# Attention and a Fourier mixing layer in one kernel: the end of an attention unit in three steps, and the sums of stage 2 on GpSimd

## The chip, the core and the metric

The kernel runs on one core of a Trainium2 chip. The metric is the device time of one execution in microseconds; the kernel before has a median of 2939.95 us in 3 runs (2938.06 to 2941.15). The engines of the core are called PE (TensorE: matmuls), DVE (VectorE), ACT (ScalarE), POOL (GpSimd) and SP (the engine whose queue issues the DMAs here).

## The reference

Two layers on inputs of 2048 positions and 1024 columns; their outputs stand side by side.

```python
# A: 32 heads of 32 columns; one k and one v for all heads
q = heads(x @ wq); k = x @ wk; v = x @ wv
p = softmax(einsum("bhqd,bkd->bhqk", q, k) * 32 ** -0.5)
a_out = concat_heads(einsum("bhqk,bkd->bhqd", p, v)) @ wo
# B: Real(DFT_seq(DFT_hidden(x)))
a = einsum("bsd,ed->bse", x, dft_hid_re); b = einsum("bsd,ed->bse", x, dft_hid_im)
b_out = einsum("ts,bse->bte", dft_seq_re, a) - einsum("ts,bse->bte", dft_seq_im, b)
return concatenate([a_out, b_out], axis=-1)
```

## The kernel before

Every large product in float32 is made of three matmuls in the type fp32r: each operand is split into a high part (a cast) and a low part (operand less its high part), and the product is high x high, high x low, low x high. The names are `mh` and `ml` for the left operand, `rh` and `rl` for the right one. Such a product of 128 x 512 over 1024 rows is a group (class `Group`): 24 matmuls into one PSUM bank `psb`, and at its end `post`.

All groups stand in one list: the projections to k, v and q, stage 1 of the Fourier layer (along the hidden axis), stage 2 (along the sequence) and the projection with `wo`. The function `take(n)` issues the next n matmuls of this list; they fill PE while the attention runs. Around them the planner (`pump`, class `Line`) issues loads on SP, sums of two left operands on GpSimd (`comb`, tiles `m`), casts and subtractions, each a fixed number of matmuls ahead of its use.

Stage 2 uses a scheme with seven products in place of eight (`PRODUCTS`), each in two halves of eight groups. The first half is put aside in a tile `h` by ACT. At the end of a group of the second half (`post` in `stage2`, line 467) DVE adds the PSUM bank to `h`; then `h` is added to or subtracted from each partial result `y` that was loaded from DRAM (line 472), and SP stores it (line 473). A product has one or two such targets beside new ones; 48 of the 56 groups have at least one sum.

The attention runs in 32 units (a block of 512 queries, four heads) of 32 steps. In the main loop (line 680) a step n does four things. `score_step`: two matmuls give 128 x 1024 scores in PSUM (`pss`, two buffers), DVE reduces them to the negative maximum of each row (`nm`), and ACT takes the exponential of the scores one step back, of which only the row sum is kept, and which frees the buffer. `expo`: two matmuls give transposed scores (`pst`, one buffer), ACT writes their exponential to `p`. Every eighth step `pv`: 16 matmuls multiply `p` with `v` into a PSUM bank, and DVE adds it to `ov`. `level`: `take` of so many matmuls that the filling runs out evenly. The last of a unit's four `pv` (lines 623 to 634) also ends the unit: `ov` is multiplied by 1/sum (`rb`), cast to the high part `oh`, and the low part `ol` is the difference; SP stores both for the projection with `wo`.

Each engine works in the order of the program. `Ordered` keeps that order, so a step's place in the code is its place in every engine's queue. The buffers touched here: `ov`, `oh`, `ol` and `rb` one each, `y` four, `h` eight (one for each group of a half), `m` three and two.

Of the kernel before, what the change touches and what calls it, by code (L numbers as in the profile page):

```python
# [8 lines left out]
F32 = mybir.dt.float32  # L9
# [59 lines left out]
def tile_kernel(ctx: ExitStack, tc, xT, wq, wkv, wo, xbT, wT, cT, out):  # L69
# [3 lines left out]
    dve = Ordered(tc, nc.vector)  # L73
    gp = Ordered(tc, nc.gpsimd)
    sp = Ordered(tc, nc.sync)
# [9 lines left out]
    oh_d = [dram.tile([NG, P, W], F32, name=f"oh_{b}") for b in range(NQ)]  # L85
    ol_d = [dram.tile([NG, P, W], F32, name=f"ol_{b}") for b in range(NQ)]
# [27 lines left out]
    def move(q, to, of):  # L114
        q.dma_start(to.bitcast(F32), of.bitcast(F32))
# [152 lines left out]
    def bank(name, open_=False):  # L268

        b = 1 - cur["bank"] if cur["bank"] is not None else int(used[1] < used[0])  # L270
        cur["at"] += 1
        used[b] = cur["at"]
        if open_:
            cur["bank"] = b
        return ps_b[b].tile([P, W], F32, name=name)
# [40 lines left out]
    def aside():  # L316

        j = pos["fill"] % 24
        if pos["fill"] >= len(groups) * 24 or j == 0:
            return  # L320
        if j < 6:
            take(6 - j)
        elif j > 17:
            take(24 - j)
# [32 lines left out]
    ready = set()  # L357
# [73 lines left out]
    def right_of(k, s):  # L431
        assert (k, s) in ready
        return NAMES[k][s]

    def stage2():
        seen, total = {}, {}
        for _, _, outs in PRODUCTS:
            for t, e, _ in outs:
                total[t, e] = total.get((t, e), 0) + 1
        for mt, nt, outs in PRODUCTS[1:] + PRODUCTS[:1]:  # L440
            for half in range(2):
                R = [Item([(lambda s=s, nt=nt: right_of(tuple(nt), s), 1)]) for s in range(half * 8, half * 8 + 8)]
                for k in range(8):
                    left = []
                    for q in range(2):
                        s0 = half * 8 + q * 4
                        left.append(Item([(lambda a=a, k=k, s0=s0: cT[a[0], a[1] * 8 + k, :, s0:s0 + 4], a[2]) for a in mt]))
                    if half == 0:
                        def post(ps, k=k):
                            hs[k] = hp.tile([P, W], F32, name=f"h{k}")  # L450
                            act.activation(hs[k], ps, AF.Copy)
                        yield Group(left, R, post)
                        continue
                    ys = []
                    plan = []
                    for t, e, sg in outs:
                        n = seen.get((t, e, k), 0)
                        seen[t, e, k] = n + 1
                        it = None
                        if n:  # L460
                            it = Item([(lambda t=t, e=e, k=k: y_d[t][e][k], 1)])
                            ys.append(it)
                        r0 = (t * 8 + k) * P
                        to = out[r0:r0 + P, D + e * W:D + (e + 1) * W] if n + 1 == total[t, e] else y_d[t][e][k]
                        plan.append((sg, it, to))

                    def post(ps, k=k, plan=plan):
                        h = hs[k]
                        dve.tensor_add(h, h, ps)
                        for sg, it, to in plan:  # L470
                            if it is not None:
                                (dve.tensor_add if sg > 0 else dve.tensor_sub)(it.y, it.y, h)
                                sp.dma_start(to, it.y)
                            elif sg > 0:
                                sp.dma_start(to, h)
                            else:
                                o = op.tile([P, W], F32, name="qh")
                                act.activation(o, h, AF.Copy, scale=-1.0)
                                sp.dma_start(to, o)
                    yield Group(left, R, post, ys=ys)  # L480


# [41 lines left out]
    units = [(b, g) for b in range(NQ) for g in range(NG)]  # L524
    SU = 32
    LEAD = 12
    total = SU * len(units)
    qst, nm, ls, lse, pt, ov, rb, pend = ({} for _ in range(8))

    def open_unit(u):  # L530
        b, g = units[u]
        assert ("q", b, g) in ready
        q = qsp.tile([P, 4, W], F32R, name="qst")
        gp.memset(q[96:P].bitcast(F32), 0.0)
        for r, src in enumerate((qh_d, ql_d, qh_d)):
            move(sp, q[r * DH:(r + 1) * DH], src[b][g].rearrange("(h d) c -> d h c", d=DH))
        qst[u] = q
        nm[u] = sm.tile([P, 2, NC], F32, name="nm")
        ls[u] = sm.tile([P, 2, NC], F32, name="ls")

    def scores(s):
        u, r = divmod(s, SU)
        i, j = divmod(r, 2)
        h, t = divmod(i, 4)
        ps = ps_s.tile([P, 2 * W], F32, name="pss")
        for a in range(2):
            k0 = (2 * j + a) * W
            te.matmul(ps[:, a * W:(a + 1) * W], qst[u][:, h, t * P:(t + 1) * P], kst[:, k0:k0 + W], start=True, stop=True)
        dve.tensor_reduce(nm[u][:, j, i:i + 1], ps, axis=AX.X, op=ALU.max, negate=True)
        pend[s] = ps  # L550

    def row_sums(s):
        if s not in pend:
            return
        ps = pend.pop(s)
        u, r = divmod(s, SU)
        i, j = divmod(r, 2)
        act.activation(ps, ps, AF.Exp, bias=nm[u][:, j, i:i + 1], accum_out=ls[u][:, j, i:i + 1])
# [9 lines left out]
    def lse_1b(u):  # L568
        act.activation(lse[u][1], lse[u][1], AF.Exp)
# [30 lines left out]
    def expo(n):  # L600
        u, r = divmod(n, SU)
        c, hp_ = divmod(r, 2)
        if hp_ == 0:
            pt[u, c] = pp.tile([P, 4, W], F32, name="p")
        ps = ps_t.tile([P, 2, W], F32, name="pst")
        for a in range(2):
            te.matmul(ps[:, a], kst[:, c * P:(c + 1) * P], qst[u][:, 2 * hp_ + a], start=True, stop=True)
        act.activation(pt[u, c][:, 2 * hp_:2 * hp_ + 2], ps, AF.Exp)

    def pv(u, k):  # L610

        aside()
        ps = bank("psb")
        for c in range(4 * k, 4 * k + 4):
            for h in range(4):
                te.matmul(ps[h * DH:(h + 1) * DH], v[:, c], pt[u, c][:, h], start=c == 4 * k, stop=c == 4 * k + 3)
        if k == 0:
            ov[u] = onp.tile([P, W], F32, name="ov")
            dve.tensor_copy(ov[u], ps)
        else:  # L620
            dve.tensor_add(ov[u], ov[u], ps)
        cur["at"] += 1
        if k == NC // 4 - 1:
            b, g = units[u]
            hi_ = onp.tile([P, W], F32R, name="oh")
            lo_ = onp.tile([P, W], F32R, name="ol")
            dve.tensor_mul(ov[u], ov[u], rb[u])
            dve.tensor_copy(hi_, ov[u])
            dve.tensor_sub(lo_, ov[u], hi_.bitcast(F32))
            lse["out"] = hi_, lo_  # L630
            if u + 1 < len(units):
                move(sp, oh_d[b][g], hi_)
                move(sp, ol_d[b][g], lo_)
            ready.add(("o", b, g))

    def score_step(s):

        if s < total:
            u, r = divmod(s, SU)
            if r == SU - 6 and u + 1 < len(units):  # L640
                open_unit(u + 1)
            scores(s)
        row_sums(s - 1)
        u, e = divmod(s - SU, SU)
        if 0 <= u < len(units):
            if e == 1:
                lse_1(u)
            elif e == 2:
                lse_1b(u)
            elif e == 3:  # L650
                lse_2(u)
            elif e == 5:
                lse_3(u)
# [26 lines left out]
    for n in range(total):  # L680
        u, r = divmod(n, SU)
        if n == total - 12:
            w1 = wo_set(1)
            add([o_group(NQ - 1, t, e, ws) for e, ws in ((0, w0), (1, w1)) for t in range(4)])
        score_step(n + SU + LEAD)
        expo(n)
        if r == 16:
            inverse(u)
        if r % 8 == 0 and n:
            pv(*divmod(n // 8 - 1, 4))  # L690
        level(n + 1)


    last = groups[len(groups) - 8:]
    take((len(groups) - 8) * 24 - pos["fill"] - 12)
    pv(len(units) - 1, 3)
    hi7, lo7 = lse["out"]
    take((len(groups) - 8) * 24 - pos["fill"])

# [58 lines left out]
```

## Time and profile before

| | us |
|---|---|
| median of 3 runs | 2939.95 |
| the profiled execution | 2945.72 |
| its span, first to last instruction | 2943.9 |
| PE busy | 2862.6 (97%) |
| ACT busy | 2273.9 (77%) |
| DVE busy | 2043.3 (69%) |
| POOL busy | 379.2 (13%) |

The granted clock of TensorE was 0.998 of full speed over the span. The profile gives each instruction's engine, start and duration, and for idle time what ended it. Matmuls overlap in a pipeline and their ends are modelled, so the time from one matmul's start to the next one's start tells more than their busy time. All instructions of the kernel are recorded on one line (L50, the helper that keeps the order), so they are told apart by their tiles. About 180 us are projections to k, v and the first q before the attention begins; stage 1 runs from 550 to 1170 us, stage 2 from there to 2620 us, the projection with `wo` after it.

### The profile page before, as it was taken

The page shows a single profiled execution, that of the slowest core. Times are in us where ns is not written, and L with a number is a line of the kernel's source. Part 1 is how long each engine was busy: PE and PEld are TensorE (multiplying, and loading weights), DVE is VectorE, ACT ScalarE, POOL GpSimd, SP SyncE. Part 2 cuts the span into 40 slices and gives each one's busy share as a digit, 9 for nine tenths or more (in the row PEclk, how much of TensorE's full clock was granted, in tenths as well). Part 3 has the DMA queues.
Part 4 walks back from the last instruction along what each step waited for, and adds up shares of the span by engine and source line. Part 5 has one row for each costly group of instructions (what it writes and reads, how often), then busy time and mean ns, then how long its engine had stood idle before and what let it go on. Part 6 is the DMA issues. An engine that isn't in the chain of part 4 may idle for free.

```text
span 2943.9 us, 39970 instructions
## 1 busy us (share of the span) xinstructions
PE 2862.6 (97%) x14096; PEld 1953.1 (66%) x14096; DVE 2043.3 (69%) x2657; ACT 2273.9 (77%) x3342; POOL 379.2 (13%) x278
## 2 busy tenths in 40 slices
PE   8999999999999999999999999999999999999999
PEld 5776666666666666666666666666666666666666
DVE  6866677655555556787788787788888787875511
ACT  4688888787888888877877877878878778788851
POOL 0000000011122223222222220002222200000000
PEclk9999999999999999999999999999999999999999
DMA  8854555455666767445355453254454432454455
GB/s 303 281 195 162 171 171 188 157 174 178 197 209 210 230 212 225 125 149 157 104 166 156 131 168 112 94 173 139 133 158 139 137 119 84 144 160 128 133 145 175
DMA packets 318025, 485.03 MB, mean 165 GB/s; under 512 B 33664, under 2 KB 98688, under 8 KB 317824
## 3 DMA queue, kind: packets, MB, share of 16 engines
q1 hardware_dynamic: 317824, 482.48, 51.4%
q8 instruction: 111, 1.82, 0.2%
q14 instruction: 90, 0.74, 0.1%
HBM read 351.54 MB, written 129.76 MB: 163 GB/s over the span
## 4 chain that ended last, share of the span: by engine, by line
PE 55%; DVE 10%; ACT 5%; issue 1%; DMA 1%; POOL 0%; SPq 0%; ACTq 0%; POOLq 0%; DVEq 0%
PE psb L50 36%; PE pst L50 11%; PE pss L50 9%; DVE nm L50 4%; ACT p L50 2%; ACT pss L50 2%; DVE ov L50 1%; DVE ml L50 1%; DVE y L50 1%; DVE h L50 1%; DVE ol L50 1%; DVE rl L50 1%; DMA m<-in_cT_dram 0%; DVE oh L50 0%; DVE mh L50 0%
## 5 line engine op out<-in xcount | busy, mean ns | idle before, releaser
L50 DVE TENSOR_REDUCE nm<-pss 128x1 f32<-128x1024 f32 x1024 | 1249.1, 1221 | 377.9 <-PE pss L50 374.9
L50 ACT ACTIVATE p<-pst 128x1024 f32<-128x1024 f32 x1024 | 1054.1, 1029 | 387.5 <-PE pst L50 381.1
L50 ACT ACTIVATE pss<-pss,nm 128x1024 f32<-128x1024 f32 x1024 | 1118.5, 1092 | 172.8 <-DVE nm L50 165.1
L50 PE MATMUL psb<-rh,mh 128*128 128x512 f32 (+1 forms) x1916 | 755.4, 394 | 8.6 <-ACT rh L50 8.2
L50 PE MATMUL psb<-rh,ml 128*128 128x512 f32 (+1 forms) x1916 | 755.6, 394 | 0.1
L50 PE MATMUL psb<-rl,mh 128*128 128x512 f32 (+1 forms) x1916 | 754.9, 394 | 0.3 <-DVE rl L50 0.3
L50 PE MATMUL pss<-kst,qst 128*128 128x512 f32 x2048 | 661.6, 404 | 33.5 <-ACT pss L50 32.4
L50 PE MATMUL pst<-qst,kst 128*128 128x512 f32 x2048 | 665.2, 406 | 24.4 <-ACT p L50 23.2
L50 PEld LDWEIGHTS pss<-kst,qst 128*128 128x128 f32 x2048 | 369.1, 188 | 237.3 <-issue 87.2
L50 PEld LDWEIGHTS pst<-qst,kst 128*128 128x128 f32 x2048 | 364.3, 188 | 176.1 <-ACT p L50 101.8
L50 PE MATMUL psb<-p,v 128*32 128x512 f32 x4096 | 466.0, 595 | 1.2 <-DVE h L50 1.2
L50 PEld LDWEIGHTS psb<-rh,mh 128*128 128x128 f32 (+1 forms) x1916 | 359.4, 188 | 96.4 <-ACT rh L50 8.7
L50 PEld LDWEIGHTS psb<-rl,mh 128*128 128x128 f32 (+1 forms) x1916 | 359.3, 188 | 87.0 <-DVE rl L50 1.6
L50 PEld LDWEIGHTS psb<-rh,ml 128*128 128x128 f32 (+1 forms) x1916 | 359.3, 188 | 86.0 <-issue 0.6
L50 POOL TENSOR_TENSOR m<-m,m 128x512 f32<-128x512 f32 x160 | 218.2, 1364 | 872.7 <-DMA m<-in_cT_dram 681.4
L50 PEld LDWEIGHTS psb<-p,v 128*32 128x32 f32 x4096 | 120.0, 109 | 277.3 <-issue 264.8
L50 DVE TENSOR_TENSOR ov<-ov,psb 128x512 f32<-128x512 f32 x96 | 66.0, 688 | 289.3 <-PE psb L50 289.3
L50 ACT ACTIVATION_READ_ACCUMULATOR pss<-pss,nm 128x1 f32 x1024 | 214.5, 210 | 0.0
L50 DVE TENSOR_TENSOR ml<-m,mh 128x512 fp32r<-128x512 f32 (+1 forms) x274 | 208.4, 761 | 4.2 <-ACT mh L50 3.9
L50 POOL MEMSET qst<- 32x2048 f32 x32 | 58.0, 1817 | 843.4 <-PE pst L50 676.9
L50 DVE TENSOR_TENSOR rl<-r,rh 128x512 fp32r<-128x512 f32 x196 | 145.6, 744 | 4.2 <-ACT rh L50 3.2
L50 DVE CAST mh<-m 128x512 fp32r<-128x512 f32 x267 | 132.1, 495 | 7.6 <-DMA m<-in_wq_dram 6.1
(63 smaller groups left out, 698.1 us busy)
## 6 DMA issues: line engine op xcount, KB each, us to landing
m<-in_cT_dram SPq DMA_DIRECT2D x384, 256.0 KB, 3.6
r<-r SPq DMA_DIRECT2D x112, 256.0 KB, 3.7
mh<-xb SPq DMA_DIRECT2D x96, 256.0 KB, 3.9
ml<-xb SPq DMA_DIRECT2D x96, 256.0 KB, 4.2
y<-y SPq DMA_DIRECT2D x96, 256.0 KB, 2.9
y<-r SPq DMA_DIRECT2D x80, 256.0 KB, 2.9
r<-y SPq DMA_DIRECT2D x80, 256.0 KB, 2.0
qst<-qh SPq DMA_DIRECT2D x64, 256.0 KB, 5.8
```

Source lines behind the costliest of these rows:

```text
L50: return lambda *a, **k: self.tc.keep_in_program_order(f(*a, **k))
```

## The change

In `pv` the three instructions at a unit's end are no longer issued at once: they go into a list `ends`, and the main loop issues one of them in each of the next three steps, behind `score_step`. The stores and the mark that the unit is ready go with the last. After the loop what is left is issued at once (the last unit). In `post` of stage 2 the sums into `y` go from DVE to GpSimd.

```diff
@@ post of stage2
-                                (dve.tensor_add if sg > 0 else dve.tensor_sub)(it.y, it.y, h)
+                                (gp.tensor_add if sg > 0 else gp.tensor_sub)(it.y, it.y, h)
                                 sp.dma_start(to, it.y)
@@ pv
             hi_ = onp.tile([P, W], F32R, name="oh")
             lo_ = onp.tile([P, W], F32R, name="ol")
-            dve.tensor_mul(ov[u], ov[u], rb[u])
-            dve.tensor_copy(hi_, ov[u])
-            dve.tensor_sub(lo_, ov[u], hi_.bitcast(F32))
             lse["out"] = hi_, lo_
-            if u + 1 < len(units):
-                move(sp, oh_d[b][g], hi_)
-                move(sp, ol_d[b][g], lo_)
-            ready.add(("o", b, g))
+
+            def low():
+                dve.tensor_sub(lo_, ov[u], hi_.bitcast(F32))
+                if u + 1 < len(units):
+                    move(sp, oh_d[b][g], hi_)
+                    move(sp, ol_d[b][g], lo_)
+                ready.add(("o", b, g))
+
+            ends.append(lambda: dve.tensor_mul(ov[u], ov[u], rb[u]))
+            ends.append(lambda: dve.tensor_copy(hi_, ov[u]))
+            ends.append(low)
@@ main loop
         score_step(n + SU + LEAD)
+        if ends:
+            ends.pop(0)()
         expo(n)
@@ after the main loop
     pv(len(units) - 1, 3)
+    while ends:
+        ends.pop(0)()
     hi7, lo7 = lse["out"]
```

PE's order of instructions stays as it was. On DVE, at the end of the 22nd unit (2050 us in the trace of before), the order was this:

```order
L50 TENSOR_TENSOR ov<-ov,psb 128x512
L50 TENSOR_TENSOR ov<-ov,rb 128x512
L50 CAST oh<-ov 128x512
L50 TENSOR_TENSOR ol<-ov,oh 128x512
L50 TENSOR_REDUCE nm<-pss 128x1
L50 TENSOR_TENSOR ml<-m_18112,mh 128x512
L50 TENSOR_REDUCE nm<-pss 128x1
```

With the change it is this (a number behind `m` or `r` only tells one tile from another):

```order
L50 TENSOR_TENSOR ov<-ov,psb 128x512
L50 TENSOR_REDUCE nm<-pss 128x1
L50 TENSOR_TENSOR ov<-ov,rb 128x512
L50 TENSOR_TENSOR ml<-m_18112,mh 128x512
L50 TENSOR_REDUCE nm<-pss 128x1
L50 CAST oh<-ov 128x512
L50 CAST mh<-m_18157 128x512
L50 CAST rh<-r_18155 128x512
L50 TENSOR_REDUCE nm<-pss 128x1
L50 TENSOR_TENSOR ol<-ov,oh 128x512
```

The next reduction stands right behind the add into `ov`, and each of the three instructions stands behind one of the next reductions, ahead of that step's conversions.

At the end of the first group of stage 2 that has a sum (1490 us in the trace of before), DVE had:

```order
L50 TENSOR_TENSOR h_12427<-h_12427,psb 128x512
L50 TENSOR_TENSOR y_13229<-y_13229,h_12427 128x512
L50 TENSOR_TENSOR ml<-m_13198,mh 128x512
L50 TENSOR_REDUCE nm<-pss 128x1
L50 CAST mh<-m_13252 128x512
```

On GpSimd the change puts the sum between two sums of left operands:

```order
 L50 TENSOR_TENSOR m_13154<-m_13154,m_13156 128x512
 L50 TENSOR_TENSOR m_13198<-m_13198,m_13200 128x512
+L50 TENSOR_TENSOR y_13229<-y_13229,h_12427 128x512
 L50 TENSOR_TENSOR m_13252<-m_13252,m_13254 128x512
 L50 TENSOR_TENSOR m_13329<-m_13329,m_13331 128x512
+L50 TENSOR_TENSOR y_13354<-y_13354,h_12565 128x512
```

The row of `y` leaves DVE, where `ml` now follows `h`; on GpSimd the sum waits for `h`, and `m_13252`, which DVE casts two rows behind `ml`, stands behind the sum.

## Rows read from the trace of the kernel before

**Rows 1.** The page: its busy sums, and DVE in 40 slices
```profile
PE 2862.6 (97%) x14096; PEld 1953.1 (66%) x14096; DVE 2043.3 (69%) x2657; ACT 2273.9 (77%) x3342; POOL 379.2 (13%) x278
...
DVE  6866677655555556787788787788888787875511
```

**Rows 2.** Timeline at a unit's end: start, duration, engine, instruction, [idle before]
```profile
2049.46 0.69 DVE L50 TENSOR_TENSOR ov<-ov,psb 128x512 f32<-128x512 f32 x1 [3.08 <-PE psb L50]
...
2050.19 0.69 DVE L50 TENSOR_TENSOR ov<-ov,rb 128x512 f32<-128x512 f32 x1
...
2050.91 0.43 DVE L50 CAST oh<-ov 128x512 fp32r<-128x512 f32 x1
...
2051.37 0.69 DVE L50 TENSOR_TENSOR ol<-ov,oh 128x512 fp32r<-128x512 f32 x1
2051.53 0.63 PE L50 MATMUL pss<-kst,qst 128*128 128x512 f32 x2
...
2051.98 1.22 DVE L50 TENSOR_REDUCE nm<-pss 128x1 f32<-128x1024 f32 x1
2051.99 0.63 PE L50 MATMUL pst<-qst,kst 128*128 128x512 f32 x2
...
2053.30 1.09 ACT L50 ACTIVATE pss<-pss,nm 128x1024 f32<-128x1024 f32 x1 [1.71 <-DVE nm L50]
2053.38 0.39 PE L50 MATMUL psb<-rh,mh 128*128 128x512 f32 x1
...
2053.61 0.39 PE L50 MATMUL psb<-rl,mh 128*128 128x512 f32 x1
...
2054.55 0.73 PE L50 MATMUL pss<-kst,qst 128*128 128x512 f32 x2 [0.56 <-ACT pss L50]
...
2055.47 0.73 PE L50 MATMUL pst<-qst,kst 128*128 128x512 f32 x2 [0.18 <-ACT p L50]
```

**Rows 3.** Timeline of PE at the first and the thirtieth unit end
```profile
249.11 0.40 PE L50 MATMUL psb<-rh,ml 128*128 128x512 f32 x1
249.81 0.73 PE L50 MATMUL pss<-kst,qst 128*128 128x512 f32 x2 [0.30 <-ACT pss L50]
...
2743.21 0.39 PE L50 MATMUL psb<-rh,mh 128*128 128x512 f32 x1
2744.15 0.73 PE L50 MATMUL pss<-kst,qst 128*128 128x512 f32 x2 [0.56 <-ACT pss L50]
```

**Rows 4.** Groups by form: count | busy us, mean ns | idle before
```profile
L50 POOL TENSOR_TENSOR m<-m,m 128x512 f32<-128x512 f32 x160 | 218.2, 1364 | 872.7 <-DMA m<-in_cT_dram 681.4 <-DVE nm L50 70.9 <-DVE rl L50 31.1
...
L50 POOL TENSOR_TENSOR y<-y,qh 128x512 f32<-128x512 f32 x48 | 62.5, 1302 | 246.1 <-ACT qh L50 232.9 <-DMA qst<-qh 13.1
...
L50 DVE TENSOR_TENSOR y<-y,h 128x512 f32<-128x512 f32 x64 | 47.2, 758 | 1.6
```

**Rows 5.** Timeline in stage 2: additions on GpSimd, and a group's end with one sum
```profile
1484.10 1.23 DVE L50 TENSOR_REDUCE nm<-pss 128x1 f32<-128x1024 f32 x1
...
1484.59 1.30 POOL L50 TENSOR_TENSOR m<-m,m 128x512 f32<-128x512 f32 x1 [5.42 <-DMA m<-in_cT_dram]
...
1489.87 0.68 DVE L50 TENSOR_TENSOR h<-h,psb 128x512 f32<-128x512 f32 x1
...
1490.58 0.69 DVE L50 TENSOR_TENSOR y<-y,h 128x512 f32<-128x512 f32 x1
...
1490.67 1.75 POOL L50 TENSOR_TENSOR m<-m,m 128x512 f32<-128x512 f32 x1 [4.78 <-DVE h L50]
...
1491.19 1.78 DVE L50 TENSOR_TENSOR ml<-m,mh 128x512 fp32r<-128x512 f32 x1
...
1492.89 1.21 DVE L50 TENSOR_REDUCE nm<-pss 128x1 f32<-128x1024 f32 x1
...
1494.54 0.39 PE L50 MATMUL psb<-rh,ml 128*128 128x512 f32 x1
...
1495.45 0.73 PE L50 MATMUL pss<-kst,qst 128*128 128x512 f32 x2 [0.53 <-ACT pss L50]
```

More of the change, by code (lines that the diff above doesn't have):

```diff
@@ L528, in tile_kernel @@
     qst, nm, ls, lse, pt, ov, rb, pend = ({} for _ in range(8))
+    ends = []
     def open_unit(u):
```

## The prediction

> **What bounds the kernel now.** I read the page first: PE is busy 97% of the span, DVE 69%, and DVE's tenths rise from 5 and 6 in the middle to 7 and 8 in the second half of the slices [rows 1]. PE's order of instructions is the same in both kernels, so only PE's waits can change the end. The second view was the timeline about a unit's end. At 2049.46 DVE adds the last product into `ov`, and then does product, cast and subtraction one behind the other; the reduction of the next scores, whose matmuls were long done, starts at 2051.98, 1.83 us after the add's end at 2050.15. ACT's exponential over those scores stands idle 1.71 us for it, and then PE stands, because both buffers of `pss` are taken [rows 2]. I count PE's loss from start to start, since the ends of matmuls are modelled: a `psb` matmul starts 0.23 after the one before (2053.38 to 2053.61), but `pss` starts 0.94 after it (2053.61 to 2054.55), 0.71 too late; `pst` follows `pss` after 0.46 when nothing waits (2051.53 to 2051.99), here after 0.92, another 0.46 [rows 2]. A unit's end costs PE 1.17 us there.
>
> **Unit ends.** The same picture stands at 30 of the 32 ends; the last two lie where the work of filling has ended or nearly so. The part before `pss` is 0.47 at the first (249.11 to 249.81, less 0.23) and 0.71 at the thirtieth (2743.21 to 2744.15) [rows 3]; over the thirty it lies between 0.47 and 1.71, mean 0.83. The part before `pst` is the 0.46 of the worked case each time. So 30 x (0.83 + 0.46) = 38.6 us of PE's time hang on these three DVE instructions.
> The change keeps the add in its place and puts the reduction straight behind it; product (0.69), cast (0.43) and subtraction (0.69) [rows 2] come one each behind the next three reductions. The 1.83 us of delay thereby falls to nothing at the reduction where it hurts. What can come late instead is the next one: a step lasts 2.31 us on PE (2051.53 to 2053.84, if the next `pss` had followed at 0.23), a reduction and the largest piece take 1.22 + 0.69 = 1.91, and 0.40 is left for the conversions of the filling work, a cast and a subtraction (0.43 + 0.69 = 1.12) in a full step. A full step then ends 0.72 late. The reduction that came 1.83 late cost 0.71 before `pss`, so about 1.12 of lateness is free; one full step is within that, two in a row are not quite. I take nine tenths of the 38.6, 35 us. The bounds: nothing (the lateness only moves) and all 38.6, and I take a value near the upper one because the piece and its delay are seen in the rows, and the thirty ends are alike in stages where DVE has room and where it has little.
> The two stores `oh` and `ol` move on SP's queue behind the loads that the next three steps issue; that lets those loads go out before SP waits for `oh`. What reads them comes units later, so I cost it at nothing; if they came late, output groups near the end would wait.
>
> **The sums into y.** Of 56 groups that end a half in stage 2, 48 have such a sum: 32 one, 16 two, 64 in all. On DVE one takes 758 ns on average; GpSimd has the like addition in stage 1 at 1302 ns, and its additions of `m` take 1364 [rows 4]. DVE is relieved of 64 x 0.758 = 48.5 us, GpSimd takes on 64 x 1.30 = 83 us, which its 13% share [rows 1] holds with ease. What this is worth on PE is seen at the groups' ends: at 1489.87 `h` is added, `y` follows, then `ml`, and the reduction behind them starts at 1492.89; `pss` then starts 0.91 after the matmul before it, 0.68 too late [rows 5]. Read so, the PE starts in the 3 to 7 us behind the 48 additions of `h` are late by 27 us in all, between nothing and 1.77 us each. Part of that belongs to the add of `h`, which stays, and to `ml`.
> For `ml` shows the price of GpSimd: begun at 1491.19 beside GpSimd's addition of 1490.67, it took 1.78 us, where the subtraction of the same form at the unit's end took 0.69 [rows 2, 5], and it ended half a microsecond behind GpSimd's. GpSimd's addition itself, begun while DVE summed `y`, took 1.75 instead of 1.30. The reduction of 1484.10, beside GpSimd's addition of 1484.59, kept its 1.23 [rows 5]. So two additions from SBUF stand in each other's way, and a reduction from PSUM does not.
> The Trainium skill, page "SBUF — State Buffer", section "Who interferes with whom", says that a DVE instruction with two SBUF inputs contends with a GpSimd instruction that reads SBUF, and that the one that issues second waits for the whole instruction of the first, while a reduction never contends. By that rule a sum on GpSimd locks DVE's subtractions and casts for longer than the sum took on DVE. The durations of rows 5 agree with it, and it makes the slower rival below possible.
> After the change a sum begins as `h` ends, at once or behind the `ml` that DVE starts first; its 1.30 us lie beside the reduction (1.21) where that comes next, and then DVE loses little. Where casts and subtractions come next, DVE loses what it had saved. And GpSimd keeps its order: the addition of the next `m` now stands behind the sum, and the cast that needs this `m` stands in DVE's order before the next reduction. At ten places DVE's order reads `h`, `ml`, reduction, cast of just that `m`: `ml` and reduction end 0.69 + 1.21 = 1.90 after `h`, GpSimd's sum and addition end 0.69 + 1.30 + 1.30 = 3.29 after it, so the cast waits 1.4 us and the next reduction is 1.8 us late with the cast, like a unit's end: 10 x 1.29 = 13 us. The bounds of this part are thus 27 us gained and 13 us lost, with more in the slower rival. The nearest row is the one of 1490, where relief and new wait about cancel; I take 6 us gained. SP's stores of `y` go out 0.6 us or more later each, with the loads behind them, which are issued several us ahead of their use: nothing.
>
> **The sum.** 35 + 6 = 41 us off the profiled execution's 2945.72 (span 2943.9 and 1.8 around it): 2904.7. The median of the runs lies 5.8 us below that execution, so 2939.95 - 41 = 2899.
>
> **Rivals.**
> 1. The sums on GpSimd give nothing back and the wait for `m` takes their place at the ten places: 35 - 13 = 22 us gained, 2918. For it: the order and the 1.78 us of `ml`. Against: at these places PE pays already today.
> 2. The unit's pieces only move the lateness where DVE is full. 17 of the 30 ends lie in stage 2, so 17 x 1.29 = 22 us stay: 38.6 - 22 = 17 us gained, 2923. For it: DVE's 7 and 8 tenths there. Against: with the wait gone the reduction has 1.12 us of free lateness in each step.
> 3. Both parts give all: 38.6 + 27 = 66, 2874. Against: the add of `h` stays on DVE.
> 4. Rivals 1 and 2 together: 17 - 13 = 4 us gained, which cannot be told from no change (0.2%, 5.9 us, is about what a measurement can tell).
> 5. Slower, by GpSimd's hold on DVE: at each of the 48 places two GpSimd additions in a row (2.60 us) keep DVE's subtraction or cast standing, and the next reduction is 2.60 late, 1.48 beyond the free 1.12, plus 0.46 before `pst`: 48 x 1.94 = 93 us, less the 27 paid there now and the 35 of the unit ends: 31 us slower, 2971. It decides from the point where these places cost over 35 us more than now, 0.73 us each. For it: `ml` of rows 5. Against: at 28 of the 48 places the order has an instruction that reads PSUM right behind `h` (19 times the reduction, which was not held up).
>
> **Chances.** My forecast 0.65, with a range of its own of 2888 to 2910 (unit ends 30 to 38, sums -1 to 14); rival 1 0.14; rival 2 0.07; rival 3 0.05; rival 4 0.04; rival 5 0.05. The range that leaves out rivals 4 and 5, half of rival 3 and part of rival 2 is 2882 to 2923. Faster: 0.65 + 0.14 + 0.07 + 0.05, less 0.01 for their edges, 0.90; no change 0.05; slower 0.05.
>
> **What would show it.** Unit ends right: in the timeline the reduction starts straight behind the add into `ov`, ACT's 1.71 is gone, and PE's `pss` and `pst` follow at 0.23 and 0.46 there; wrong if the same waits stand two or three steps later. Sums right: GpSimd's `y` at about 1.3 us 64 times, reductions behind `h` earlier, few casts of `m` that wait for GpSimd; wrong if idle time of DVE put down to GpSimd's `m` grows to over 10 us, or if the subtractions' mean rises. The forecast fails if PE's busy share does not rise or DVE's waits turn up as waits of PE elsewhere.

## The result, and the profile after

The changed kernel takes 2895.55 us in the median of 4 runs (2893.22 to 2897.75), against 2940.55 of the kernel before on the same occasion: a ratio of 0.9848, 95% interval [0.9831, 0.9865], or 45 us less. The forecast was 2899. The profiled execution took 2893.22 (span 2891.4).

The busy sums of the page, to be read against [rows 1]: PE is busy 23 us less for the same matmuls (a pair that waits is recorded as 0.73 us, one that runs on as 0.63), DVE is relieved of 48, GpSimd took on 89.

```profile
PE 2839.5 (98%) x14096; PEld 1957.6 (68%) x14096; DVE 1995.0 (69%) x2593; ACT 2279.2 (79%) x3342; POOL 467.8 (16%) x342
```

Who waited for whom, first in the kernel before (total us, times, longest):

```profile
ACT pss L50 <- DVE nm L50: 165.1, 145, 4.0
...
PE pss L50 <- ACT pss L50: 32.4, 49, 2.4
```

and after the change:

```profile
ACT pss L50 <- DVE nm L50: 95.2, 111, 3.5
...
DVE mh L50 <- POOL m L50: 15.1, 11, 2.5
...
PE pss L50 <- ACT pss L50: 11.7, 16, 1.9
```

ACT waits 70 us less for DVE's reductions, and PE 21 us less for the buffers of `pss`; one wait has grown, DVE's for GpSimd's `m`, from 1.3 us in 2 times to 15.1 in 11.

The end of the same unit as in [rows 2], in the timeline of the changed kernel (start, duration, engine, instruction):

```profile
2011.06 0.69 DVE L50 TENSOR_TENSOR ov<-ov,psb 128x512 f32<-128x512 f32 x1 [3.08 <-PE psb L50]
...
2011.69 1.22 DVE L50 TENSOR_REDUCE nm<-pss 128x1 f32<-128x1024 f32 x1
...
2012.83 0.68 DVE L50 TENSOR_TENSOR ov<-ov,rb 128x512 f32<-128x512 f32 x1
2012.89 0.39 PE L50 MATMUL psb<-rl,mh 128*128 128x512 f32 x1
...
2013.08 1.08 ACT L50 ACTIVATE pss<-pss,nm 128x1024 f32<-128x1024 f32 x1
2013.12 0.63 PE L50 MATMUL pss<-kst,qst 128*128 128x512 f32 x2
...
2013.58 0.63 PE L50 MATMUL pst<-qst,kst 128*128 128x512 f32 x2
...
2014.03 1.22 DVE L50 TENSOR_REDUCE nm<-pss 128x1 f32<-128x1024 f32 x1
...
2015.16 0.42 DVE L50 CAST oh<-ov 128x512 fp32r<-128x512 f32 x1
2015.20 0.40 PE L50 MATMUL psb<-rl,mh 128*128 128x512 f32 x1
...
2015.43 0.63 PE L50 MATMUL pss<-kst,qst 128*128 128x512 f32 x2
...
2015.90 0.63 PE L50 MATMUL pst<-qst,kst 128*128 128x512 f32 x2
...
2017.30 0.69 DVE L50 TENSOR_TENSOR ol<-ov,oh 128x512 fp32r<-128x512 f32 x1
```

The reduction begins at 2011.69, as the add into `ov` ends, not 1.83 us after it. ACT goes on to the scores at 2013.08 without idle time. PE starts `pss` 0.23 after the matmul before it, in this step and the next (2012.89 to 2013.12, 2015.20 to 2015.43), and `pst` 0.46 and 0.47 behind. Product, cast and subtraction stand behind one reduction each (2012.83, 2015.16, 2017.30) and nobody waits for them. In the 3 to 7 us behind the add into `ov` no start of PE is late at any of the thirty ends, where before each lost 0.93 us or more.

The first group of stage 2 with a sum, the place of [rows 5], has come out as the order promised, and not to the good:

```profile
1466.66 0.68 DVE L50 TENSOR_TENSOR h<-h,psb 128x512 f32<-128x512 f32 x1
...
1467.25 0.69 DVE L50 TENSOR_TENSOR ml<-m,mh 128x512 fp32r<-128x512 f32 x1
...
1467.42 1.68 POOL L50 TENSOR_TENSOR y<-y,h 128x512 f32<-128x512 f32 x1 [11.48 <-DVE h L50]
...
1467.86 1.22 DVE L50 TENSOR_REDUCE nm<-pss 128x1 f32<-128x1024 f32 x1
...
1469.06 2.53 POOL L50 TENSOR_TENSOR m<-m,m 128x512 f32<-128x512 f32 x2
...
1470.38 1.50 DVE L50 CAST mh<-m 128x512 fp32r<-128x512 f32 x1 [1.30 <-POOL m L50]
...
1471.79 1.21 DVE L50 TENSOR_REDUCE nm<-pss 128x1 f32<-128x1024 f32 x1
...
1474.36 0.73 PE L50 MATMUL pss<-kst,qst 128*128 128x512 f32 x2 [0.33 <-ACT pss L50]
...
1475.39 0.73 PE L50 MATMUL pst<-qst,kst 128*128 128x512 f32 x2 [0.30 <-ACT p L50]
```

`h` ends at 1467.34, GpSimd's sum begins at 1467.42 and is held up by DVE's `ml` (1.68 us, not 1.30), then come two additions of `m` (2.53 us for both). DVE has done its reduction by 1469.0, stands idle 1.30 us for the first `m`, and the cast then takes 1.50 us beside the second addition where others take 0.42. The next reduction is late, and PE waits 0.33 before `pss` and 0.30 before `pst`.

Left operands' subtractions and casts on DVE, first before the change (count | busy us, mean ns | idle before):

```profile
L50 DVE TENSOR_TENSOR ml<-m,mh 128x512 fp32r<-128x512 f32 x272 | 207.6, 763 | 3.3 <-ACT mh L50 3.0
...
L50 DVE CAST mh<-m 128x512 fp32r<-128x512 f32 x267 | 132.1, 495 | 7.6 <-DMA m<-in_wq_dram 6.1 <-POOL m L50 1.3 <-PE psb L50 0.2
```

and after, with GpSimd's sums:

```profile
L50 DVE TENSOR_TENSOR ml<-m,mh 128x512 fp32r<-128x512 f32 x272 | 197.3, 726 | 3.6 <-ACT mh L50 3.2
L50 DVE CAST mh<-m 128x512 fp32r<-128x512 f32 x267 | 145.2, 544 | 21.6 <-POOL m L50 15.1 <-DMA m<-in_wq_dram 6.0 <-DMA ql<-ql 0.3
...
L50 POOL TENSOR_TENSOR y<-y,h 128x512 f32<-128x512 f32 x64 | 91.7, 1443 | 564.8 <-DVE h L50 505.9 <-DMA rb<-r 43.7 <-DMA m<-in_cT_dram 15.2
```

A sum takes 1443 ns with its waits for DVE, more than the 1302 of [rows 4]. The subtractions have become shorter in the mean, the casts longer by 49 ns, with 14 us more of idle time before them. Counted over the DVE instructions that ran beside the 64 sums, these took 6.5 us more in all than the medians of their kinds, where DVE was relieved of 48; 45 of the sums lay beside a reduction.

### The profile page after: what moved, and what is told of

The parts are those of the page before. It is cut to its first block, busy times and chain, and to the rows that moved or that the text cites. A ratio compares the mean times of both kernels' runs of the same rounds, so it can differ in the third digit from the quotient of the medians.

```text
span 2891.4 us, 39967 instructions
## 1 busy us (share of the span) xinstructions
PE 2839.5 (98%) x14096; PEld 1957.6 (68%) x14096; DVE 1995.0 (69%) x2593; ACT 2279.2 (79%) x3342; POOL 467.8 (16%) x342
## 4 chain that ended last, share of the span: by engine, by line
PE 45%; issue 6%; DVE 4%; ACT 3%; DMA 3%; POOL 2%; SPq 0%; POOLq 0%; ACTq 0%
PE psb L50 29%; PE pst L50 9%; PE pss L50 8%; DVE nm L50 2%; DMA y<-y 1%; ACT p L50 1%; POOL y L50 1%; ACT pss L50 1%; DVE mh L50 1%; DMA m<-in_cT_dram 1%; SPq L50 0%; DVE ml L50 0%; DMA y<-r 0%; DVE rl L50 0%; POOL m L50 0%
## 5 line engine op out<-in xcount | busy, mean ns | idle before, releaser
L50 DVE TENSOR_REDUCE nm<-pss 128x1 f32<-128x1024 f32 x1024 | 1250.6, 1222 | 361.9 <-PE pss L50 358.8
L50 PE MATMUL pss<-kst,qst 128*128 128x512 f32 x2048 | 657.5, 402 | 12.4 <-ACT pss L50 11.7
L50 DVE TENSOR_TENSOR ml<-m,mh 128x512 fp32r<-128x512 f32 (+1 forms) x274 | 198.1, 723 | 4.0 <-ACT mh L50 3.6
L50 POOL TENSOR_TENSOR y<-y,h 128x512 f32<-128x512 f32 x64 | 91.7, 1443 | 564.8 <-DVE h L50 505.9
L50 DVE CAST mh<-m 128x512 fp32r<-128x512 f32 x267 | 145.2, 544 | 21.6 <-POOL m L50 15.1
```

Of the source, the lines that this page charges most:

```text
L50: return lambda *a, **k: self.tc.keep_in_program_order(f(*a, **k))
```

## The experiments

All ratios are to the kernel before on the same occasion, from 5 rounds each; 0.001 is 3 us. The changed kernel has 0.9848. An interval reaches some 4 us to either side, so the difference of two ratios is open by some 6 us. e6 and e9 add `h` twice and e10 stores zeros, so their Fourier output is not the kernel's; they stand here for their time.

| run | what it is | median us | ratio, 95% interval |
|---|---|---|---|
| e1 | unit ends spread, sums on DVE | 2905.48 | 0.9877 [0.9862, 0.9892] |
| e2 | sums on GpSimd, unit ends in one piece | 2933.19 | 0.9968 [0.9955, 0.9980] |
| e3 | e1 with the three pieces as a lump behind the reduction | 2920.49 | 0.9923 [0.9909, 0.9936] |
| e4 | changed kernel, sums issued behind the next m | 2889.88 | 0.9821 [0.9808, 0.9835] |
| e5 | changed kernel, pieces ahead of the reductions | 2904.93 | 0.9877 [0.9863, 0.9890] |
| e6 | changed kernel, every sum twice | 2917.84 | 0.9921 [0.9908, 0.9935] |
| e7 | e4, preparation of 1/sum in two steps | 2887.02 | 0.9815 [0.9802, 0.9829] |
| e8 | changed kernel, groups with one sum back on DVE | 2895.78 | 0.9843 [0.9829, 0.9856] |
| e9 | e4, every sum twice | 2897.62 | 0.9851 [0.9838, 0.9865] |
| e10 | changed kernel, three memsets behind each sum | 2921.32 | 0.9932 [0.9920, 0.9945] |
| e11 | e7, second sum of a group 12 matmuls later | 2890.20 | 0.9822 [0.9808, 0.9835] |

**e1 and e2: each part alone.** e1 is the changed kernel with

```diff
-                                (gp.tensor_add if sg > 0 else gp.tensor_sub)(it.y, it.y, h)
+                                (dve.tensor_add if sg > 0 else dve.tensor_sub)(it.y, it.y, h)
```

and e2 the kernel before with the opposite edit.

> The unit's end in three steps, the sums into y left on DVE. Theory A (the unit ends carry the gain): 35 to 38 us faster than before, about 2903; the starts of PE behind the 30 unit ends are no longer late. Theory B (the two parts need each other: with y on DVE the pieces only move the lateness in stage 2): 17 us faster, about 2923, with PE late two or three steps behind the 17 unit ends of stage 2.

> The sums into y on GpSimd, the unit's end left in one piece. Theory A: 6 to 10 us faster than before, about 2932, and the unit ends cost PE 1.29 us each as before. Theory B: close to nothing, 2940, since the gain of the sums only comes with room at the unit ends. Rival (GpSimd holds DVE up): slower than before.

e1 gained 36 us and e2 9; their sum, 45.6, is the whole change's 44.7. Theory A holds: the parts do not need each other, and the unit ends carry four fifths. In e1 PE's waits for `pss` are already nearly those of the changed kernel, with DVE nearly as loaded as before (2032 us busy):

```profile
PE pss L50 <- ACT pss L50: 13.2, 17, 2.7
```

In e2 the unit ends cost what they did: in the 3 to 7 us behind the thirty adds into `ov` PE starts 41 us late in all, 42 in the kernel before, none in the changed one.

**e3: is it the spreading, or only the place behind the reduction?**

```diff
-            ends.append(lambda: dve.tensor_mul(ov[u], ov[u], rb[u]))
-            ends.append(lambda: dve.tensor_copy(hi_, ov[u]))
-            ends.append(low)
+            def all_three():           # product, cast and low() in one step
...
+            ends.append(all_three)
```

> Sums on DVE; the unit's three instructions go together, as one lump, behind the next reduction, and are not spread. If what counts is only that the first reduction goes ahead of them: as e1, about 2903. If the lateness allowed in a step is about 1.12 us, as I worked out: the second reduction comes late by the lump less the room of a step, 1.83 - 0.40 and more where conversions stand there, so that about half of the ends lose again some 0.5 to 1.3 us: about 12 us less gain than e1, 2915.

By the ratios it loses 14 us of e1's gain. At a unit's end in stage 2 the timeline shows the old wait one step later:

```profile
1685.16 0.69 DVE L50 TENSOR_TENSOR ol<-ov,oh 128x512 fp32r<-128x512 f32 x1
...
1686.11 0.42 DVE L50 CAST rh<-r 128x512 fp32r<-128x512 f32 x1
...
1686.44 1.22 DVE L50 TENSOR_REDUCE nm<-pss 128x1 f32<-128x1024 f32 x1
...
1687.76 1.09 ACT L50 ACTIVATE pss<-pss,nm 128x1024 f32<-128x1024 f32 x1 [1.41 <-DVE nm L50]
...
1689.01 0.73 PE L50 MATMUL pss<-kst,qst 128*128 128x512 f32 x2 [0.40 <-ACT pss L50]
```

The lump's subtraction is followed by the step's two casts, the reduction begins at 1686.44, ACT has stood idle 1.41 us, and PE waits 0.40 before `pss`. So the place gives some three fifths of the gain and the spreading the rest.

**e5: how much lateness of a reduction is free?** The list is served ahead of `score_step`, so that each piece stands in front of its step's reduction.

```diff
-        score_step(n + SU + LEAD)
         if ends:
             ends.pop(0)()
+        score_step(n + SU + LEAD)
         expo(n)
```

> As the changed kernel, but each of the three pieces stands ahead of its step's reduction and not behind it: each reduction of three is then late by 0.69, 0.43 and 0.69 us. If about 1.12 us of lateness of a reduction is free, as I worked out from the rows of before: no more than 3 us slower than the changed kernel, some 2897, and no waits of PE at the unit ends. If every delay of a reduction costs PE: 30 x (0.2 to 0.5 us) in each of up to three steps, 15 us or more slower, 2910.

It came out between the two, 9 us slower than the changed kernel. Counted by PE's starts, the excess stands in the steps behind a unit's end: in steps 2 to 7 of the units PE starts 24 us late in all, 14 in the changed kernel. An end early in the run shows how:

```profile
329.38 0.69 DVE L50 TENSOR_TENSOR ov<-ov,rb 128x512 f32<-128x512 f32 x1
...
329.99 1.22 DVE L50 TENSOR_REDUCE nm<-pss 128x1 f32<-128x1024 f32 x1
...
331.30 1.09 ACT L50 ACTIVATE pss<-pss,nm 128x1024 f32<-128x1024 f32 x1 [0.52 <-DVE nm L50]
...
332.40 1.02 ACT L50 ACTIVATE p<-pst 128x1024 f32<-128x1024 f32 x1
...
333.31 1.08 ACT L50 ACTIVATE pss<-pss,nm 128x1024 f32<-128x1024 f32 x1
...
333.50 0.71 PE L50 MATMUL pst<-qst,kst 128*128 128x512 f32 x2
```

The product stands first, the reduction is 0.6 us late, ACT idles 0.52 us, and from there on it has no idle time: its step takes 2.0 us (331.30 to 333.31) and PE's 2.2 to 2.3, so it makes up little in a step. PE then waits within the pair of `pst` (0.71 us where the pair takes 0.63), since `pst` has one buffer that ACT frees. My 1.12 us of free lateness counted the way over `pss` alone.

**e6, e9 and e10: what does a sum on GpSimd cost?** e6 issues each sum twice in the changed kernel, e9 does the same in e4.

```diff
                                 (gp.tensor_add if sg > 0 else gp.tensor_sub)(it.y, it.y, h)
+                                (gp.tensor_add if sg > 0 else gp.tensor_sub)(it.y, it.y, h)
```

> As the changed kernel, but each of the 64 sums into y is issued twice in a row on GpSimd, so that y gets h twice (the output of the Fourier layer is another one). It takes the suspected price of GpSimd (1.3 to 1.4 us each, in which DVE's subtractions and casts stand, and the next m comes late) once more. If a sum on GpSimd costs PE little: up to 5 us slower, 2900. If GpSimd's hold on DVE is what eats the gain of the sums: 64 x some 0.4 us, 25 us or more slower, 2920.

A second sum costs 22 us over the 64, 0.34 us each, nearly what I had for GpSimd's hold on DVE. But the trace of e6 names another cause beside it. (It is of e6's slowest run, 2928.34 us at a granted clock of 0.994; the other four took 2916 to 2921 at 0.996 to 0.999.)

```profile
DVE mh L50 <- POOL m L50: 36.4, 18, 5.3
...
PE pss L50 <- ACT pss L50: 32.6, 19, 4.3
```

DVE's wait for `m` has gone from 15.1 to 36.4 us, and PE's for `pss` from 11.7 to 32.6. Whether the order on GpSimd or its hold on DVE is the price was left to e9 and e10.

> The version with the sums behind the addition of m, each sum issued twice (y gets h twice, another output for the Fourier layer). The second sum cost the changed kernel 22 us, 0.35 us each. If that was the order on GpSimd (the next m late, and DVE's cast waiting for it): 5 to 8 us slower than the version with single sums, 2897. If it was GpSimd's hold on DVE's subtractions and casts: again about 20 us, 2910.

```profile
DVE mh L50 <- POOL m L50: 2.3, 4, 1.0
```

With `m` issued first the second sum costs 9 us over e4 by the ratios, not 22. The wait for `m` is all but gone, though GpSimd does as much work as in e6. So some 13 of the 22 us were the order, which the four intervals leave open by some 8; the other 9 are what is left for the hold and for the later stores of `y`, which these runs do not part.

e10 puts three memsets behind each sum:

```diff
+                                for _ in range(3):
+                                    gp.memset(it.y, 0.0)
```

> As the changed kernel, but behind each sum stand three memsets of y on GpSimd in place of a second sum (y is stored as zeros, another output for the Fourier layer): about the same time on GpSimd, but nothing read. If the price of the second sum (22 us) is GpSimd's order: as the doubled sums, 2918. If it is the hold on DVE's subtractions, which need both inputs from SBUF: less, by up to half, some 2907, and the means of ml and rl stay at 726 and 731 ns.

In time it is as slow as e6, and three memsets take 1.6 us in the mean, somewhat more than a second sum. But a part of its time is neither order nor hold. Its rows:

```profile
1474.33 1.50 DVE L50 CAST mh<-m 128x512 fp32r<-128x512 f32 x1 [3.06 <-POOL m L50]
...
1478.31 0.88 PE L50 MATMUL pss<-kst,qst 128*128 128x512 f32 x2 [2.08 <-ACT pss L50]
...
1480.36 0.63 PE L50 MATMUL psb<-rh,mh 128*128 128x512 f32 x1
1480.79 0.63 PE L50 MATMUL psb<-rl,mh 128*128 128x512 f32 x1
...
1484.14 0.68 DVE L50 TENSOR_TENSOR ml<-m,mh 128x512 fp32r<-128x512 f32 x1
1484.22 1.69 POOL L50 MEMSET y<- 128x512 f32 x3
```

The cast at 1474.33 waited 3.06 us for `m` behind sum and memsets, and took 1.50 beside the next addition. PE then stood 2.08 us before `pss`, and behind that its matmuls start 0.43 us apart, not 0.23: from 1478.7 to 1482.1 the granted clock was 0.50, the lower of its two levels (1.2 GHz). Between 180 us and 2850 e10's trace has six such stretches, five of them just behind a place where PE started over 2 us late; they cost about 10 us by the starts of PE. e6's trace has seven (about 8 us), the changed kernel's none. All five runs of e10 have a granted clock of 0.994 to 0.996, while three of e6's have 0.998 or 0.999 and took 2916 to 2918. So e10 without the slow stretches would take some 2911, an estimate: 15 us above the changed kernel and not 25, between the two expectations.

Where PE is late speaks for the order all the same. In the 12 us behind the add of `h`, at the groups with one sum, PE is 20 us later in e6 and 16 in e10 than in the changed kernel, the slow stretches included; at those with two sums it is no more than 2 us later.

The hold is not nothing in e10 either. The subtraction at 1484.14 kept its 0.68 beside the memsets, as every subtraction did that lay beside memsets alone, but the nine casts that did so took 0.46 to 0.84 us, not 0.42: 3 us of DVE's time in all. The means of `ml` and `rl`, 741 and 721 ns, are above and below the 726 and 731 I had expected to see unmoved; the difference to e6 (745 and 751) is too small to make a price.

**e8: which sums gain?**

```diff
+                        two = sum(it is not None for _, it, _ in plan) == 2
...
-                                (gp.tensor_add if sg > 0 else gp.tensor_sub)(it.y, it.y, h)
+                                eng = gp if two else dve
+                                (eng.tensor_add if sg > 0 else eng.tensor_sub)(it.y, it.y, h)
```

> As the changed kernel, but only the 16 groups with two sums have them on GpSimd; the 32 with one sum keep it on DVE. If the gain of the sums comes from both alike (32 of 64 sums each): half of the 10 us is lost, 2900. If the wait of casts for m behind the sum eats the gain of the groups with one sum (those with two have no additions of m around them, but for three): the same as the changed kernel, 2895, or faster.

The same time as the changed kernel, within the intervals: the 32 groups with one sum gain nothing on GpSimd, the 16 with two gain all. Read from PE's starts in the 12 us behind the add of `h`: at the groups with two sums PE is 13.1 us late in e1 and 5.1 in the changed kernel, at those with one 22.9 and 24.8. The wait for `m` has gone with the groups of one sum:

```profile
DVE mh L50 <- POOL m L50: 3.5, 2, 2.5
```

**e4, e7 and e11: a better order.** In e4 the sums of a group are put off until the planner has issued the next addition of `m` (the list `later` is served right behind it); the count that lets the next `y` be loaded (`yused`) moves with them:

```diff
...
+                        def sums():
+                            for sg, it, to in plan:
+                                if it is not None:
+                                    (gp.tensor_add if sg > 0 else gp.tensor_sub)(it.y, it.y, h)
+                                    sp.dma_start(to, it.y)
+                                    yused[0] += 1
+                        later.append((pos["fill"], sums))
...
```

> As the changed kernel, but at each group's end the sum into y is issued on GpSimd behind the addition of the next m (and behind the loads and conversions of that moment), where it stood ahead of it. If the casts that wait for GpSimd's m (15 us in 11 waits after the change, none of note before) cost PE: 5 us faster than the changed kernel, about 2890. If DVE's room covers them: the same, 2895.

By the ratios 8 us faster than the changed kernel, at the edge of what the intervals tell apart; by PE's starts the gain lies at the groups with one sum (7 us less late, read as in e8), and those with two are as they were. At the first group with a sum GpSimd now adds `m` 5 us before `h`, and the cast goes through in 0.41 us without waiting, beside the sum's end:

```profile
1464.27 1.59 POOL L50 TENSOR_TENSOR m<-m,m 128x512 f32<-128x512 f32 x1 [5.69 <-DMA m<-in_cT_dram]
...
1469.68 1.68 POOL L50 TENSOR_TENSOR y<-y,h 128x512 f32<-128x512 f32 x1 [3.82 <-DVE h L50]
...
1471.27 0.41 DVE L50 CAST mh<-m 128x512 fp32r<-128x512 f32 x1
```

e7 takes e4 and splits another lump of DVE, the five small instructions of `lse_2`:

```diff
         dve.tensor_add(l, d[:, 0], d[:, 1])
+        lse[u] = m, l, m2
+
+    def lse_2b(u):                     # called one step later
+        m, l, m2 = lse[u]
         dve.tensor_copy(m2[:, 0].bitcast(F32R), m)
...
```

> The version with the sums behind the addition of m, and the five small DVE instructions that prepare a unit's 1/sum (about 1.1 us in one step) split over two steps: two in the one, three in the next. If what holds for the unit's end holds for this lump too: 3 to 6 us faster than that version, about 2885. If 1.1 us is within the free lateness: the same, 2890.

2 us by the ratios, less than the intervals tell apart: inconclusive, and nearer to the second expectation. Of all versions it has the lowest time, 54 us below the kernel before, though the ratios of e4 and e11 lie within its interval.

e11 puts off the second sum of a group by 12 more matmuls (`pos["fill"] + 12 * i`).

> The version with the row sums in two steps, and in groups with two sums the second one 12 matmuls later, so that the two no longer hold GpSimd for 2.6 us in a row. If two sums in a row still keep DVE's casts standing: 2 to 4 us faster, 2884. If not: the same, 2887.

No gain, 2 us to the other side, within the intervals.

## Why the prediction was right, point by point

**Unit ends: right in place and size.** Forecast 35 us, measured 36 (e1). The step that thirty losses of 1.29 us in the mean (0.93 to 2.2, not equal) hang on three DVE instructions was seen in the rows, and the losses are gone in the rows after. Rival 2, that in stage 2 the lateness only moves, is refuted by e1.

**The free lateness of 1.12 us: wrong.** The step compared the reduction's 1.83 us with PE's 0.71 before `pss`. It left out that ACT, once late, stays late for steps, and that `pst` has one buffer. e5 shows that three reductions late by 0.43 to 0.69 us cost 9 us. The forecast did not suffer, since in the changed kernel the pieces stand behind the reductions, and what they add there fits in DVE's room: in the 7 to 17 us behind the thirty adds into `ov` PE is late by 9 us before and by 10 after. For e3 the same figure happened to give nearly the right size (12 expected, 14 measured).

**The sums: 6 us forecast, 9 measured, and the split was not seen.** The row of 1490 stood for groups with one sum, and for them the prediction's words hold: relief and new wait cancel (e8). The gain is that of the groups with two sums, where no addition of `m` stands behind (but for three), and DVE is relieved of 1.4 us at a time. Rival 1 was a real mechanism: its ten places became 11 waits of 15.1 us, and taking them away gave 8 us (e4), where I had priced them at 13. By the prediction's own sign this part should have failed: DVE's idle time for `m` grew past the 10 us that it named. It gained all the same: at the groups with one sum the wait ate no more than DVE's relief gave, and those with two gained 8 us by PE's starts. So the 6 us, taken from a row of the groups that gain nothing, came near the 9 by luck.

**GpSimd's hold on DVE: there, but not the price I feared.** "SBUF — State Buffer" of the Trainium skill, section "Who interferes with whom", says that a DVE instruction with two SBUF inputs contends with a GpSimd instruction that reads SBUF, not with one that only writes it. The rows agree: `ml` of 1.78 us in [rows 5], `ml` of 0.68 beside memsets in e10. But the slower rival built on it fell. With 64 more additions on GpSimd the subtractions became shorter in the mean (726 ns, 763 before), not longer; what grew is the casts, by 49 ns, and the hold of all 64 sums came to 6.5 us of DVE's time. The casts grew mostly beside work that GpSimd had before: beside the 160 additions of `m` casts of 128x512 lost 14 us before and 29 after, subtractions 34 and 17. In e1 it is 16 and 32, in e2 27 and 18, so the sums moved those additions to where the casts stand. The dearer thing, by e6 and e9, was the order of GpSimd's own queue.

**The sum.** 41 us forecast, 45 measured: 1 us of the difference by the unit ends, 3 by the sums.

## What to carry to other kernels

Where one engine's in-order queue feeds a chain to the bottleneck, look at what stands ahead of the instruction that the chain waits for: a lump that costs the engine nothing on average cost PE 1.3 us each time, and putting the urgent instruction first gave three fifths, spreading the rest the remainder. Work that is moved to an idle engine takes a place in that engine's order too; put it behind what others wait for, not where the old code stood (8 us here). Count losses of a pipelined engine from start to start, place by place: 30 losses of 1.3 us were worth more than any share of busy time told.

## What was not expected of the hardware

The prediction had GpSimd hold casts as well as subtractions, but its rows showed only a subtraction. A cast from float32 to fp32r on DVE, 0.42 us alone, takes 1.50 us beside an addition on GpSimd that begins at about the same time (1470.38 in the changed kernel, 1474.33 in e10): GpSimd went first and the cast lost more than a whole subtraction would have cost. A GpSimd instruction that only writes held casts too, and no subtraction. Beside the memsets of `qst` (32x2048, 1.81 us), which both kernels have, a cast took up to 2.11 us in the kernel before (at 1380.99), and subtractions kept 0.68. Reductions from PSUM were untouched (mean 1221 ns before, 1222 after).

PE pays for a long wait twice when its granted clock falls behind it: in e10 2.08 us of standing at 1478.31, then matmuls 0.43 us apart, not 0.23, until 1482.
